# S4 convolution with a gated FFN on Trainium2: the first transform of the convolution in eight array tiles instead of four

## The chip, the cores and the metric

The kernel runs on one core of one Trainium2 chip. The metric is the device time of one execution in microseconds, the median of three runs. The engines are named as in the profile: PE is TensorE (its matmuls), PEld its weight loads, DVE VectorE, ACT ScalarE, POOL GpSimd, SP SyncE, which here only issues DMAs.

## The reference

Two branches read the same normalized input; their product is added to the input.

```python
def reference(A_u, ...):                       # u: (1, 2048, 512)
    xn = _layernorm(A_u, axis=-1)
    s = _A_ref(xn, ...)                        # S4: y = causal convolution over the sequence
    g = _silu(_B_ref(xn, w1, b1, w2, b2))      # gelu(xn @ w1 + b1) @ w2 + b2, 512 -> 1792 -> 512
    return A_u + s * g

def _A_ref(u, ...):
    P = jnp.exp(logdA[:, :, None] * l[None, None, :])
    K = jnp.einsum("dn,dnl,dn->dl", Cc, P, dB).real      # a kernel of 2048 taps for each of 512 channels
    ...                                                  # rfft of K and u, padded to 4096, product, irfft
    return y + u * Dskip
```

## The kernel before

The sequence has 2048 rows of 512 channels; channels are handled in four batches `b` of 128. Three pieces of work are interleaved.

*The start.* `prologue()` loads the first rows of the input and the first weights, computes the time steps, and normalizes. While loads are under way PE multiplies the identity with itself (`warm`, L431, called with 6 and with 25, each a matmul of 128x128 by 128x128 into a bank of tag `f1`). The first work of PE that others wait for are the transposes `xT` of the normalized rows (`ln_turn`, L369); ACT and DVE split them into a high and a low part (`xh`, `xl`), and with these the first layer of the FFN begins (`first_start`, L266).

*The middle.* A long table of tokens, `ORDER`, sets by hand the order in which the FFN's matmuls (`f` L256 to L258, `z` L295 to L297, in a form of fp32 that takes one pass) and the generation of the convolution's taps follow one another. The taps are summed by `gen_sum` (L656), calls with 32 columns of weights and 64 moving columns in four tiles of columns.

*The end.* The convolution is done with two short transforms in place of the FFT: `first_dft` (over 32 points), `second_dft` (L883, over 64), a product, and the way back (`back_dft` L918, `swing` L936, `last_dft` L975). `first_dft` is called with a batch `b`, `u` (0 the input, 1 the taps) and a half `h`, 16 calls in all, here called groups. Its operands lie with 32 rows for each of four sub-batches `g`, so a call of `PE.matmul` has 32 rows, and the four `g` use four tiles of rows of the array and four PSUM banks. The stationary operand is the data (two channels by 64 points: 128 columns), the moving one the constant `fc` (64 columns). ACT, at the first four groups DVE too, copies the four banks out as `X` (`first_out`, L870).

The groups of batch 0 are strung between the last parts of the FFN by a string of tokens (`F00`, `F01`, `F10`, `F11` among `S`, `L` and `A`). Those of batches 1 to 3 stand in `slot(b, g)`, eight slots for each batch: every slot has one `second_dft`, every even slot of batches 0 to 2 one group of the next batch, every odd slot from the first pair on two `back_dft`. From slot to slot PE's work is in the order of the code. Tables of the transforms (`mc`, `tcn`) are loaded by SP's queue around the start of this part.

In fp32 each call of `PE.matmul` becomes two pairs of a weight load and a matmul, so 32 calls stand as x64 in the profile.

Of the kernel before, what the change touches and what calls it, by code (L numbers as in the profile page):

```python
# [11 lines left out]
F32 = mybir.dt.float32  # L12
# [8 lines left out]
P = 128  # L21
# [12 lines left out]
TB = 4  # L34
# [138 lines left out]
def kernel(  # L173
# [5 lines left out]
    V, A, GP, PE, SY = nc.vector, nc.scalar, nc.gpsimd, nc.tensor, nc.sync  # L179
# [27 lines left out]
    fc = keep.tile([P, 2 * N1], F32, name="fc")  # L207
    ident = keep.tile([P, P], F32, name="ident")
# [6 lines left out]
    def stage_first(f):  # L215
        if f >= FA and f % 2:
            x = wka.tile([P, 2, D], F32, tag="x", name=f"ws{f}", bufs=2)
            st, raw_w[f, 1] = x[:, 0, :].rearrange("p (k m) -> p k m", k=KD), x[:, 1, :]
        else:
            st = stg.tile([P, KD, P], F32, tag="st", name=f"w1s{f}")  # L220
        raw_w[f, 0] = st
        SY.dma_start(st, w1.rearrange("(k p) f -> p k f", p=P)[:, :, f * P:(f + 1) * P])

    def stage_second(f):
        if (f, 1) not in raw_w:
            raw_w[f, 1] = stg.tile([P, D], F32, tag="st", name=f"w2s{f}")
        SY.dma_start(raw_w[f, 1], w2[f * P:(f + 1) * P, :])

    def split(f, k, other=0):
        if k == 0:  # L230
            g = f % FA
            W[f] = (wpa.tile([P, KD, P], F32R, tag=f"w1h{g}", name=f"w1h{f}"),
                    wpa.tile([P, KD, P], F32R, tag=f"w1l{g}", name=f"w1l{f}"),
                    wpa.tile([P, D], F32R, tag=f"w2h{g}", name=f"w2h{f}"),
                    wpa.tile([P, D], F32R, tag=f"w2l{g}", name=f"w2l{f}"))
        j = k % 2
        h, lo = W[f][2 * j:2 * j + 2]
        if k < 2:
            A.copy(h, raw_w[f, j])  # L239
        else:  # L240
            (GP if other else V).tensor_sub(lo, raw_w[f, j], h)  # L241

    def opened(stack, name, side, bufs=1, space=None):
        kw = {} if space is None else {"space": space}
        return stack.enter_context(tc.tile_pool(name=name, bufs=bufs, side=side, reuse_waits="tile", **kw))
# [62 lines left out]
    ps1 = opened(fa, "ps1", "left", space=PSUM)  # L308
# [5 lines left out]
    def ln_load(n):  # L314
        if n == 2:
            ln["zi"] = wka.tile([P, TB, D], F32, tag="zi", name="x23")
        if n in (2, 3):
            x = ln["zi"][:, 2 * n - 4:2 * n - 2, :]
        else:
            x = wka.tile([P, 2, D], F32, tag="x", name=f"x{n}", bufs=2)  # L320
        for j in range(2):
            SY.dma_start(x[j * 64:(j + 1) * 64], x_l[j, :, 2 * n:2 * n + 2, :])
        ln[n] = x
# [6 lines left out]
    def ln_stats(n, mv):  # L330
        for i in range(2):
            ln_stat(n, i, mv)
# [16 lines left out]
    def ln_scale(n, mv, rs):  # L349
        x = ln[n]  # L350
        for i in range(2):
            V.tensor_scalar(x[:, i, :], x[:, i, :], mv[:, i, 0:1], rs[:, i:i + 1],
                            op0=ALU.subtract, op1=ALU.mult)
# [18 lines left out]
    def ln_high(n, i, other=0):  # L372
        t, hf = divmod(n, 2)
        s = slice((2 * hf + i) * P, (2 * hf + i + 1) * P)
        if other:
            V.tensor_copy(xt[t][0][:, :, s], ln[n, i])
        else:
            A.copy(xt[t][0][:, :, s], ln[n, i])
# [30 lines left out]
    def bias_load():  # L409
        SB["b2"] = st = wka.tile([P, TB * P], F32, tag="hf", name="b2st", bufs=2)  # L410
        V.memset(st, 0.0)
        for k in (0, 32):
            A.dma_start(st[k:k + 1], b2.rearrange("(o d) -> o d", o=1))
        one = wka.tile([P, TB * P], F32, tag="hf", name="one", bufs=2)
        V.memset(one[:, :P], 1.0)
        A.activation(one[:, P:P + 1], one[:, :1], AF.Gelu_apprx_tanh)
        A.copy(ones, one[:, :P])

    def bias_high():
        A.copy(b2r, SB["b2"])  # L420

    def bias_low():
        V.tensor_sub(b2r[32:33], SB["b2"][32:33], b2r[32:33])
# [4 lines left out]
    def warm(n):  # L428
        p = ps1.tile([P, P], F32, tag="f1", name="warm", bufs=2)
        for _ in range(n):  # L430
            PE.matmul(p, ident, ident, start=True, stop=True, skip_group_check=True)  # L431

    def z_add(t, i):
        V.tensor_add(fin[t][:, i, :], zt[t + NTB][i], fin[t][:, i, :])

# [19 lines left out]
    def timestep():  # L455
        def small(tag, dt=F32):
            return par.tile([P, G], dt, tag=tag, name="sm_" + tag)

        x = small("x")
        rows = par.tile([G, P], F32, tag="pr", name="sm_rows")  # L460
        A.dma_start(rows, log_dt.rearrange("(g p) -> g p", p=P))
        yield
        p = pss.tile([P, G], F32, tag="sm", name="sm_turn")
        PE.transpose(p, rows, ident[:G, :G])
        A.copy(x, p)
        yield
        k, r, t, e = small("k"), small("r"), small("t"), small("e")
        GP.tensor_scalar(x, x, -87.0, 88.5, op0=ALU.max, op1=ALU.min)
        GP.tensor_scalar(k, x, 1.4426950408889634, MAGIC, op0=ALU.mult, op1=ALU.add)
        GP.tensor_scalar(k, k, MAGIC, 1.0, op0=ALU.subtract, op1=ALU.mult)  # L470
        GP.tensor_scalar(t, k, -0.693359375, 1.0, op0=ALU.mult, op1=ALU.mult)
        GP.tensor_add(r, t, x)
        GP.tensor_scalar(t, k, 2.12194440054690583e-4, 1.0, op0=ALU.mult, op1=ALU.mult)
        GP.tensor_add(r, r, t)
        GP.tensor_scalar(e, r, 1.0 / 5040.0, 1.0 / 720, op0=ALU.mult, op1=ALU.add)
        for c in (1.0 / 120, 1.0 / 24, 1.0 / 6, 0.5, 1.0, 1.0):
            GP.tensor_mul(e, e, r)
            GP.tensor_scalar(e, e, c, 1.0, op0=ALU.add, op1=ALU.mult)
        k2 = small("k2", I32)
        GP.tensor_scalar(k2, k, 127.0, 8388608.0, op0=ALU.add, op1=ALU.mult)  # L480
        SB["dt"] = dt = small("dt")
        GP.tensor_mul(dt, e, k2.bitcast(F32))
        yield
# [193 lines left out]
    def prologue():  # L677
        step = timestep()
        next(step)
        ln_load(0)  # L680
        ln_load(1)
        stage_first(0)
        stage_second(0)
        bias_load()
        warm(6)
        next(step)
        warm(25)
        for _ in step:
            pass
        SY.dma_start(b1s, b1.rearrange("(f p) -> p f", p=P))  # L690
        stage_first(1)
        stage_second(1)
        next(pgen[0])
        for n in range(2, 4):
            ln_load(n)
        SY.dma_start(cbs, cb)
        mv, rs = pair(0)
        bias_high()
        ln_stats(0, mv[:, 0:2, :])
        bias_low()  # L700
        ln_stats(1, mv[:, 2:4, :])
        split(0, 0)
        split(0, 1)
        ln_root(0)
        for n in range(2):
            ln_scale(n, *moments(n))
        for q, tag in enumerate(("ph", "sm", "z", "z")):
            ln_turn(q // 2, q % 2, tag)
            ln_high(q // 2, q % 2)
            ln_low(q // 2, q % 2)  # L710
            if q == 1:
                split(0, 2)
        first_start(*steps[0])

    def pair(t):
        if (t, "mv") not in ln:
            ln[t, "mv"] = wka.tile([P, TB, 2], F32, tag="mv", name=f"mv{t}", bufs=2)
            ln[t, "rs"] = wka.tile([P, TB], F32, tag="rs", name=f"rs{t}", bufs=2)
        return ln[t, "mv"], ln[t, "rs"]

    def moments(n):
        s = slice(2 * (n % 2), 2 * (n % 2) + 2)
        mv, rs = pair(n // 2)
        return mv[:, s, :], rs[:, s]

    def ln_root(n):
        ln_rsqrt(*pair(n // 2), str(n))
# [128 lines left out]
    def first_dft(b, u, h, gs):  # L856
        if b not in xf:
            xf[b] = SB["pf" if b % 2 == 0 else "pm"].tile([P, 2, 2, N1, N2], F32, tag=f"X{b % 2}", name=f"X{b}")
        src = side[b][u][h]
        ps = [bank(f"s1_{b}_{u}_{h}_{g}").rearrange("p e (i m) -> p (e i) m", m=N2) for g in gs]  # L860
        for i in range(8):
            for g, p in zip(gs, ps):
                r = slice(g * N1, (g + 1) * N1)
                PE.matmul(p[:, i, :], src[r, 2 * i:2 * i + 2, :], fc[r], start=True, stop=True, skip_group_check=True)  # L864
        fp[b, u, h] = list(zip(gs, ps))

    def first_out(b, u, h, engs=(A, A, A, A)):
# [152 lines left out]
    def slot(b, g):  # L1020
# [15 lines left out]
        if nxt and g % 2 == 0:  # L1036
            first_dft(b + 1, i // 2, i % 2, range(G))
# [57 lines left out]
    with tc.manual_schedule():  # L1095
# [9 lines left out]
        for p in "S0 F00 S1 S2 F01 S3 L0 F10 L1 A0 F11 A1 L2 L3 A2 A3".split():  # L1105
            if p[0] == "F":
                k = int(p[1]), int(p[2])
# [67 lines left out]
```

## Time and profile before

| | us |
|---|---|
| three runs | 566.54, 571.05, 569.23 |
| median | 569.23 |
| span of the profiled execution, first to last instruction | 564.4 |
| PE busy | 543.8 |
| DVE busy | 457.0 |
| ACT busy | 411.5 |
| POOL busy | 297.6 |

The page gives the profiled execution's span; the median of the runs is 4.8 us longer than it. A busy time is the union of an engine's instructions; PE's ends are modelled, so a high share says that PE always has something under way, not that it runs at its best. "issue" as the end of a wait means that no semaphore and no earlier instruction explains it. Counts of instructions (x) in rows of windows include those that reach into the window.

### The profile page before, as it was taken

The numbers are of one execution on the slowest core, as the hardware profiler recorded it, in microseconds if no ns is written. First come the engines' busy times: TensorE is split into PE (matmuls) and PEld (weight loads), VectorE is DVE, ScalarE is ACT, GpSimd is POOL, SyncE is SP. The second block draws the span as 40 slices with busy tenths as digits, with TensorE's granted clock in tenths as the row PEclk, the third lists the DMA queues.
The fourth block names the chain that finished last, engine by engine and source line by source line (L and its number), as shares of the span: only waits on it lengthen the run. The fifth ranks groups of instructions, "written<-read, shape, count | busy, mean of one in ns | idle before, by whom it ended". The sixth has DMA issues, their size and how long they took to land.

```text
span 564.4 us, 17131 instructions
## 1 busy us (share of the span) xinstructions
PE 543.8 (96%) x7179; PEld 434.5 (77%) x7179; DVE 457.0 (81%) x699; ACT 411.5 (73%) x605; POOL 297.6 (53%) x403
## 2 busy tenths in 40 slices
PE   8898999999999999999999999999999999999995
PEld 8666777777777777777777777777779998988873
DVE  6999999999899789998897976886357656867874
ACT  3587998799977998777998787897355565564542
POOL 4648378449976679969743684370320305114323
PEclk9999999999999999999999999999999999999998
DMA  8967636845192364752258138313978583625945
GB/s 188 281 193 207 186 93 201 240 141 195 54 337 74 107 193 136 257 149 58 44 186 236 52 92 107 110 38 126 362 292 78 132 135 83 174 68 126 207 109 112
DMA packets 108344, 86.91 MB, mean 154 GB/s; under 512 B 44294, under 2 KB 87562, under 8 KB 108268
## 3 DMA queue, kind: packets, MB, share of 16 engines
q1 hardware_dynamic: 97584, 65.37, 44.3%
q0 software_dynamic: 9568, 19.93, 12.0%
q8 instruction: 56, 0.92, 0.7%
q10 hardware_dynamic: 1116, 0.53, 0.4%
q14 instruction: 20, 0.16, 0.1%
HBM read 52.25 MB, written 33.55 MB: 152 GB/s over the span
## 4 chain that ended last, share of the span: by engine, by line
PE 60%; DVE 17%; issue 8%; DMA 7%; ACT 3%; SPq 3%; POOL 2%; POOLq 0%; DVEq 0%; ACTq 0%
PE z L295 8%; PE z L296 7%; PE z L297 7%; PE f L256 7%; PE f L258 7%; PE f L257 6%; PE kg L656 5%; PE s L883 4%; PE s L864 3%; PE ph L595 2%; PE sa L918 2%; DVE ra L609 2%; DVE hl L282 2%; DMA xb<-in_A_u_dram 2%; DMA gb<-gd 1%
## 5 line engine op out<-in xcount | busy, mean ns | idle before, releaser
L618 POOL TENSOR_TENSOR mm<-mm,rc 128x32 f32<-128x32 f32 (+4 forms) x150 | 115.8, 772 | 11.8
L295 PE MATMUL z<-w2h,hh 128*128 128x512 f32 x224 | 97.9, 437 | 0.0
L256 PE MATMUL f<-xh,w1h 128*128 128x512 f32 x220 | 91.4, 415 | 0.1
L297 PE MATMUL z<-w2h,hl 128*128 128x512 f32 x224 | 88.5, 395 | 0.3 <-DVE hl L282 0.3
L296 PE MATMUL z<-w2l,hh 128*128 128x512 f32 x224 | 88.6, 395 | 0.0
L258 PE MATMUL f<-xh,w1l 128*128 128x512 f32 x220 | 87.0, 395 | 1.5 <-DVE w1l L241 1.5
L257 PE MATMUL f<-xl,w1h 128*128 128x512 f32 x220 | 86.7, 394 | 0.0
L883 PE MATMUL s<-X,mc 64*64 64x128 f32 x2048 | 63.8, 272 | 1.4 <-issue 1.4
L900 DVE TENSOR_TENSOR t<-s,uh 128x512 f32<-128x512 f32 x64 | 41.0, 685 | 26.6 <-ACT uh L891 26.3
L883 PEld LDWEIGHTS s<-X,mc 64*64 64x64 f32 x2048 | 56.1, 133 | 5.6 <-issue 3.3
L615 POOL COPY mm<-rc 128x32 f32<-128x32 f32 x30 | 14.1, 469 | 81.5 <-DVE e L648 48.9
L282 DVE TENSOR_TENSOR hl<-hf,hh 128x512 fp32r<-128x512 f32 x56 | 49.9, 894 | 5.6 <-ACT hh L276 5.6
L609 DVE SCALAR_TENSOR_TENSOR ra<-ra,ph 128x512 f32<-128x512 f32 x64 | 43.6, 681 | 8.9 <-ACT ra L603 7.9
L258 PEld LDWEIGHTS f<-xh,w1l 128*128 128x128 f32 x220 | 41.3, 188 | 12.3 <-DVE w1l L241 2.4
L270 ACT ACTIVATE hf<-f,b1s 128x512 f32<-128x512 f32 x56 | 38.2, 688 | 17.1 <-DVE hl L282 9.8
L297 PEld LDWEIGHTS z<-w2h,hl 128*128 128x128 f32 x224 | 42.1, 188 | 11.1 <-DVE hl L282 1.2
L295 PEld LDWEIGHTS z<-w2h,hh 128*128 128x128 f32 x224 | 42.5, 190 | 10.5 <-issue 1.0
L256 PEld LDWEIGHTS f<-xh,w1h 128*128 128x128 f32 x220 | 41.5, 189 | 9.8 <-ACT w1h L239 0.3
L296 PEld LDWEIGHTS z<-w2l,hh 128*128 128x128 f32 x224 | 42.3, 189 | 8.2 <-DVE w2l L241 0.2
L257 PEld LDWEIGHTS f<-xl,w1h 128*128 128x128 f32 x220 | 41.4, 188 | 9.0
L641 DVE TENSOR_TENSOR e<-mm,ra 128x1024 f32<-128x1024 f32 x32 | 42.9, 1340 | 5.8 <-ACT ra L629 3.3
L870 ACT COPY X<-s 128x512 f32<-128x512 f32 x56 | 28.9, 598 | 25.3 <-PE s L864 20.2
(185 smaller groups left out, 1163.6 us busy)
## 6 DMA issues: line engine op xcount, KB each, us to landing
x<-in_A_u_dram SPq DMA_DIRECT2D x16, 256.0 KB
xs<-x SPq DMA_DIRECT2D x16, 256.0 KB
xt_h<-xh POOLq DMA_DIRECT2D x4, 1024.0 KB, 5.4
xt_l<-xl POOLq DMA_DIRECT2D x4, 1024.0 KB, 7.4
kgd<-ko SPq DMA_DIRECT2D x32, 128.0 KB
za<-zo SPq DMA_DIRECT2D x4, 1024.0 KB
xh<-xt_h POOLq DMA_DIRECT2D x4, 1024.0 KB, 6.7
xl<-xt_l POOLq DMA_DIRECT2D x4, 1024.0 KB, 10.1
```

The costliest lines, as they stand in the source:

```text
L256: PE.matmul(p, wh[:, k, :], xh[:, k, :], start=(k == 0), stop=False)
L257: PE.matmul(p, wh[:, k, :], xl[:, k, :], start=False, stop=False)
L258: PE.matmul(p, wl[:, k, :], xh[:, k, :], start=False, stop=(k == KD - 1))
L282: V.tensor_sub(hl, hf, hh)
L295: PE.matmul(z, hh[:, s], wh, start=(f0 == 0 and not rows), stop=False)
L296: PE.matmul(z, hh[:, s], wl, start=False, stop=False)
L297: PE.matmul(z, hl[:, s], wh, start=False, stop=(f0 == FA - 1))
L609: V.scalar_tensor_tensor(ra[:, 0, c], ra[:, 1, c], MAGIC, p, op0=ALU.subtract, op1=ALU.subtract)
L618: GP.tensor_mul(mv[:, :, 0:3:2, w:2 * w], mv[:, :, 0:3:2, 0:w], rc[:, 2 + 2 * i:4 + 2 * i, :].rearrange("p j c -> p c j").unsqueeze(3).to_ ...
L641: V.tensor_mul(e1, m1.unsqueeze(1).to_broadcast([P, 2, CH, N1]), ra[:, :, :, :N1])
L883: PE.matmul(p[ka * 64:(ka + 1) * 64, r, o, :, jj], mc[h, k, ((0, 2), (1, 0))[c][o], :], xf[b][h, c, :, k, :], start=(c == 0), stop=(c == 1 ...
L900: V.tensor_mul(t, p[:, i, :, 1].unsqueeze(1).to_broadcast([P, 2, 2, P]), uh)
```

## The change

The groups of `first_dft` use half the columns in each call: a call covers one channel instead of two, 64 columns of weights, and writes one half of the bank's partitions (`p[64 * e:64 * e + 64, i, :]`). Row and column tiles together make eight tiles of 32 rows by 64 columns. A group has 64 calls instead of 32. What is computed, the banks and the copies out of them are the same.

In `prologue()`, 19 of the 25 later warm-up calls are replaced by 256 calls in four tile forms (`warm_tiles`: 5 x 16 in tiles of 32x32, 8 x 8 in 64x32, 8 x 8 in 32x64, 6 x 8 in 64x32 with 128 moving columns); they write banks of tag `z`, which nobody reads.

```diff
+    def warm_tiles(rows, cols, n, k):
+        banks = [ps1.tile([P, n], F32, tag="z", name=f"warm{rows}x{cols}_{r}", bufs=TB) for r in range(P // rows)]
+        for _ in range(k):
+            for c in range(0, P, cols):
+                for r, p in enumerate(banks):
+                    s = slice(r * rows, (r + 1) * rows)
+                    PE.matmul(p[c:c + cols], ident[s, c:c + cols], ident[s, :n], start=True, stop=True, skip_group_check=True)
...
         warm(6)
         next(step)
-        warm(25)
+        warm(6)
+        warm_tiles(32, 32, 128, 5)
+        warm_tiles(64, 32, 64, 8)
+        warm_tiles(32, 64, 64, 8)
+        warm_tiles(64, 32, 128, 6)
+        warm(4)
...
         for i in range(8):
             for g, p in zip(gs, ps):
                 r = slice(g * N1, (g + 1) * N1)
-                PE.matmul(p[:, i, :], src[r, 2 * i:2 * i + 2, :], fc[r], start=True, stop=True, skip_group_check=True)
+                for e in range(2):
+                    PE.matmul(p[64 * e:64 * e + 64, i, :], src[r, 2 * i + e, :], fc[r], start=True, stop=True, skip_group_check=True)
```

The order of PE's calls at the start of the program before the change. Names are the tile that is written, then what is read; `x4` is four calls of one kind.

```order
L431 MATMUL warm_149<-ident_99 128x128 x6
L464 MATMUL sm_turn_156<-ident_99,sm_rows_129 128x4
L431 MATMUL warm_159<-ident_99 128x128 x25
L369 MATMUL xT0_0_276<-ident_99,x0_131 128x128 x4
L369 MATMUL xT0_1_283<-ident_99,x0_131 128x128 x4
L369 MATMUL xT1_0_291<-ident_99,x1_134 128x128 x4
L369 MATMUL xT1_1_298<-ident_99,x1_134 128x128 x4
```

The changed program at its start, first calls of the first tile form:

```order
L431 MATMUL warm_149<-ident_99 128x128 x6
L472 MATMUL sm_turn_156<-ident_99,sm_rows_129 128x4
L431 MATMUL warm_159<-ident_99 128x128 x6
L439 MATMUL warm32x32_0_166<-ident_99 32x128
L439 MATMUL warm32x32_1_167<-ident_99 32x128
L439 MATMUL warm32x32_2_168<-ident_99 32x128
L439 MATMUL warm32x32_3_169<-ident_99 32x128
```

And its last ones, up to the first transposes:

```order
L439 MATMUL warm64x32_1_385<-ident_99 32x128
L439 MATMUL warm64x32_0_384<-ident_99 32x128
L431 MATMUL warm_434<-ident_99 128x128 x4
L369 MATMUL xT0_0_530<-ident_99,x0_131 128x128 x4
L369 MATMUL xT0_1_537<-ident_99,x0_131 128x128 x4
```

Between the second `warm` and the transposes stand 260 calls in place of 19; the transposes themselves are the same.

PE around the first slot before the change: the end of the FFN, one `second_dft` (`s2`, 32 calls) and the beginning of a group (`s1`, 32 rows of this kind, which read `fc` and the input `in0` of batch 1).

```order
L296 MATMUL z7_3_4571<-w2l13_2978,hh_7_13_4979 128x512
L297 MATMUL z7_3_4571<-w2h13_2977,hl_7_13_4983 128x512
L883 MATMUL s2_0_0_5240<-X0_5029,mc_5006 64x2x64 x32
L864 MATMUL s1_1_0_0_0_5274<-fc_98,in0_1_5018 128x64
L864 MATMUL s1_1_0_0_1_5275<-fc_98,in0_1_5018 128x64
L864 MATMUL s1_1_0_0_2_5276<-fc_98,in0_1_5018 128x64
L864 MATMUL s1_1_0_0_3_5277<-fc_98,in0_1_5018 128x64
```

The same place after it:

```order
L897 MATMUL s2_0_0_5622<-X0_5283,mc_5260 64x2x64 x32
L878 MATMUL s1_1_0_0_0_5656<-fc_98,in0_1_5272 64x64 x2
L878 MATMUL s1_1_0_0_1_5657<-fc_98,in0_1_5272 64x64 x2
L878 MATMUL s1_1_0_0_2_5658<-fc_98,in0_1_5272 64x64 x2
L878 MATMUL s1_1_0_0_3_5659<-fc_98,in0_1_5272 64x64 x2
```

Each row of a group has become two calls of half the width; what stands before and behind the group is unmoved. On the other engines no instruction is added, removed or moved.

## The prediction

> **What bounds the kernel now.** I read first the busy times and the chain on the page, then the busy time of each engine by stage.
>
> ```profile
> PE 543.8 (96%) x7179; PEld 434.5 (77%) x7179; DVE 457.0 (81%) x699; ACT 411.5 (73%) x605; POOL 297.6 (53%) x403
> PE 60%; DVE 17%; issue 8%; DMA 7%; ACT 3%; SPq 3%; POOL 2%; POOLq 0%; DVEq 0%; ACTq 0%
> q8 instruction: 56, 0.92, 0.7%
> 0.00:12.40 12.40, 10.36 (x63) 9.93 (x63) 6.84 (x25) 3.69 (x7) 5.78 (x29) 1.00 0.86 189
> 12.40:20.40 8.00, 5.74 (x31) 4.26 (x31) 7.90 (x18) 5.54 (x11) 4.08 (x7) 1.00 0.97 268
> 40.00:392.00 352.00, 347.15 (x3337) 267.22 (x3338) 314.49 (x448) 302.30 (x406) 233.03 (x299) 1.00 0.52 146
> 392.00:411.20 19.20, 18.05 (x350) 14.50 (x348) 7.01 (x12) 7.12 (x12) 4.37 (x4) 1.00 0.90 332
> 411.20:512.60 101.40, 99.97 (x2577) 90.66 (x2576) 66.62 (x98) 58.78 (x109) 19.97 (x20) 1.00 0.59 131
> ```
>
> The columns of a stage are PE, PEld, DVE, ACT, POOL, the granted clock, the DMA share and GB/s. The first transform (L864) runs from 392 to 511, where PE is busy all but 2.6 us while DVE and ACT have a third or more of the stage free. So PE's order of work sets the end there, and also from 40 to 392. Only at the start does PE wait for others: behind the first transposes DVE is busy 7.90 of 8.00 us.
>
> Next the time line of PE, for what one group of the first transform costs and for waits that belong to no engine.
>
> ```profile
> 392.76 1.10 PE L656 MATMUL kg<-e,e 128*32 128x64 f32 x64
> 393.80 0.50 PE L295 MATMUL z<-w2h,hh 128*128 128x512 f32 x1
> ...
> 411.22 1.96 PE L883 MATMUL s<-X,mc 64*64 64x128 f32 x58
> 413.52 0.44 PE L883 MATMUL s<-X,mc 64*64 64x128 f32 x6 [0.34 <-issue]
> 413.89 2.01 PE L864 MATMUL s<-fc,in 32*128 32x64 f32 x64
> 415.84 1.96 PE L883 MATMUL s<-X,mc 64*64 64x128 f32 x58
> 418.72 2.19 PE L883 MATMUL s<-X,mc 64*64 64x128 f32 x70 [0.93 <-issue]
> 420.84 2.01 PE L864 MATMUL s<-fc,in 32*128 32x64 f32 x64
> 422.78 1.98 PE L883 MATMUL s<-X,mc 64*64 64x128 f32 x64
> 424.69 2.05 PE L918 MATMUL sa<-tcn,Y 128*128 128x128 f32 x16
> 426.67 1.98 PE L883 MATMUL s<-X,mc 64*64 64x128 f32 x64
> ```
>
> A call in fp32 is two pairs of a weight load and a matmul in the trace: 32 calls of a group are x64. From start to start a group of L864 takes 422.78-420.84 = 1.94 us, and two slots take 426.67-418.72 = 7.95 us. Twice PE stood still in the middle of L883, in a run with no semaphore of its own, "issue". The stages between these gaps, and the packets on the queue that brings instructions (windows 410.99 to 411.00 and 416.32 to 416.33), say what it waited for.
>
> ```profile
> 407.28:413.51 6.23, 5.90 (x128) 5.05 (x128) 3.46 (x6) 4.83 (x8) 0.23 (x1) 1.00 1.01 409
> 413.51:418.71 5.20, 4.27 (x128) 3.79 (x127) 1.29 (x2) 2.64 (x5) 3.27 (x5) 1.00 1.03 376
> 418.71:422.39 3.68, 3.67 (x126) 3.50 (x126) 2.50 (x4) 1.17 (x2) 0.00 (x0) 1.00 0.36 117
> 451.74:455.65 3.91, 3.91 (x138) 3.67 (x133) 2.82 (x5) 1.93 (x4) 0.00 (x0) 1.00 0.49 134
> q8 instruction: 1, 0.02, 751.2%
> q8 instruction: 1, 0.02, 673.8%
> ```
>
> From one gap's end to the next are 128 matmuls and 128 weight loads, 256 instructions. q8 moved 0.92 MB in 56 packets, 16 KB each; 56 x 256 = 14,336, and PE has 2 x 7179 = 14,358 instructions: q8 feeds PE, 256 instructions at a time. The packet that began at 411.0 took 7.512 x 16 x 0.01 = 1.20 us, was there at 412.2, and PE went on at 413.52, 1.3 us later. The one of 416.3 took 1.08, was there at 417.4, and PE went on at 418.72, again 1.3 us later. It began 2.8 us after PE had entered the block before (413.52). So only the running block and the next are held: entering one block sends for the next but one. A block of 128 pairs cannot pass faster than this round: 6.2 and 5.2 us where the DMA share is 1.0, 3.7 to 3.9 where it is 0.4 to 0.5. The present code needs 64 x 30 ns x 2 = 3.9 us for 128 pairs of L883 and L864, just at that limit.
>
> [...]
>
> **The change, part by part.** *Time of a group without the fetch.* In how tiles overlap I rely on these:
>
> ```profile
> L883 PEld LDWEIGHTS s<-X,mc x2048: 129/133/133, 411.2 to 543.1; 64*64 64x64 f32 x187
> L864 PEld LDWEIGHTS s<-fc,in x1024: 181/187/187, 392.4 to 510.6; 32*128 32x128 f32 x171
> 420.83:420.86 0.03, 0.02 (x4) 0.03 (x4) 1.00 0.00 0
> 420.86:420.94 0.08, 0.08 (x4) 0.08 (x4) 1.00 0.01 0
> ```
>
> The four row tiles get their four pairs within 0.03 us, then none starts until 420.94: PE sits out the load of 128 columns. A group is 16 rounds of 1.94/16 = 121 ns. Halving the columns shortens a load by 187-133 = 54 ns. The nearest row for small weights and the same 64 moving columns is L656: 64 pairs in 393.80-392.76 = 1.04 us, 65 ns a round. Eight pairs at 0.03/4 = 7.5 ns fit in 60 ns. So a group costs 1.04 to 1.1 us, if pairs can keep coming at 7.5 ns. No row shows eight tiles side by side; if they ran four at a time, or pairs came no faster than L656's 16 ns, 128 pairs would take 2.08. Between -0.90 and +0.14 us I take -0.85, from the 0.03 us row. DVE and ACT have the room named above, so they would not be next; instructions would.
>
> [...]
>
> *Fetch in the slots, 411 to 513 (12 groups).* Two slots hold 64+64+64+16 = 208 pairs now and 272 after, 1.63 and 2.13 blocks. At a round of 3.8 us (between 3.7 and 3.9) 2.13 blocks need 8.1 us even if work and fetch average out perfectly. They don't: the block with the 16 pairs of L918 has 112 x 0.030 + 2.0 = 5.3 us of work, and the other 1.13 blocks 4.3 us of fetch, 9.6 together. Halfway is 8.85 against 7.95, +0.9 for two slots, 12 times: **+10.8 us**. Ends: -10.2 (12 x -0.85, fetch hidden) and +19.8 (9.6 for two slots).
>
> *Fetch in the four groups before the slots, 392 to 411.* The row of this stage has 350+348 = 698 instructions in 19.2 us, 2.7 blocks at 7.0 us each, a little above the rounds of 6.2 and 5.2 us that end in and behind it. One of its four groups waited for ACT besides:
>
> ```profile
> 395.39 2.01 PE L864 MATMUL s<-fc,in 32*128 32x64 f32 x62
> 400.08 2.66 PE L864 MATMUL s<-fc,in 32*128 32x64 f32 x64 [1.09 <-ACT X L870]
> ```
>
> The groups bring 256 pairs more, two blocks: 4.7 blocks at 5.2 us are 24.6 us, +5.4, and at 6.2 us 29.3, +10. I take **+5**, by the lower row, as a block may be there at the stage's begin. Ends: -3.4 (4 x -0.85, rounds under 3.4 us) and +10.
>
> *The warm-up.* 31 calls become 272, 62 pairs 544: 964 instructions more ahead of the first transpose, on which ACT, DVE and all of the FFN wait.
>
> ```profile
> 1.51 2.93 PE L431 MATMUL warm<-ident 128*128 128x128 f32 x12 [1.51 <-POOL ident masks.py:199]
> 4.56 7.31 PE L431 MATMUL warm<-ident 128*128 128x128 f32 x50
> 12.46 2.17 PE L369 MATMUL xT<-ident,x 128*128 128x128 f32 x16 [0.59 <-DVE x L352]
> q8 instruction: 1, 0.02, 61.5%
> ```
>
> The last row is the first packet of q8, between 20.4 and 20.5; up to there PE ran (63+31) x 2 = 188 instructions. So about 190 instructions and one block of 256 are there from the start. The transposes begin behind 126 instructions now, behind 1,090 after: 126+964. That is beyond 190 + 3 x 256 = 958: three blocks must be fetched, one after the other. The first 12 pairs take 2.63 us (0.22 each), so do the 12 behind L464's successor: tiles begin at 4.56+2.6 = 7.2 and instruction 190 comes at 7.9. Then three rounds, then 132 instructions (58 tile pairs at 16 ns, 8 pairs at 0.11): 1.8 us. The transposes start at 9.7 + 3 rounds. A round is unknown here: 2.5 if the packet starts at once (1.2 + 1.3), 3.7 as at DMA share 0.36, 6.2 as at 1.01; the share at the start is 0.86 to 0.97. I take 4.5, a little under the midpoint of the last two (5.0), as the packet at 20.4 began within a few instructions of the entry that sent for it. That gives 23.2 against 12.46, +10.7, of which DVE's full stage gives next to nothing back: **+10.5**, ends +4.7 and +15.8. If the forms keep the clock from rising (0.22 us a pair at first, 7.31/50 = 0.15 in the mean of the second run), up to 3 us are added; I take none. The z banks that the tile forms write have no reader, so nobody waits for them.
>
> *Sum.* 10.8 + 5 + 10.5 = 26.3 on the span of 564.4: 590.7. The three times' median of 569.23 lies 4.8 above that span: 595.
>
> **The rivals.** (a) *Fetch is hidden, the group's 0.85 us is kept*: 16 x 0.85 = 13.6, and the tile forms at 7.5 ns a pair end near 12: 556. For it: most of the 56 blocks show no gap. Against: blocks took 12 us in the FFN and meet the limit wherever they take 4. It decides if a round in the slots falls below 7.1/2.13 = 3.3 us and the start holds more than one block. Faster; 0.08. (b) *Only the warm-up pays*: rounds near 3.5, so the slots break even: 580; 0.15. (c) *Only the stage pays*, because the start has further blocks ready: 585; 0.06. (d) *The two cancel*, slots at PE's own pace (-10.2) and the warm-up at +10.5: 569; 0.05.
>
> **How the numbers follow.** The forecast, all three terms, has 0.66. With rounds from 3.5 to 4.1 in the slots and 3.7 to 6.2 at the start it spans about 582 to 611. Down to 577 (b) and (c) lie inside; (a), (d) and a tenth of the forecast's own cases stay out, together 0.2. So 577 to 611. Slower by over 1% (about what a measurement of this kernel tells from no change): 0.66+0.15+0.06 = 0.87. Within 1%: 0.05. Faster: 0.08.
>
> **What would show it.** Right: the first transpose near 23 us with two or three "issue" gaps of 2 to 4 us in the tile forms of the warm-up; q8 with 11 or 12 packets more (3,012 instructions / 256), three of them before the first transpose; L864 in two or more pieces per group with "issue" gaps; two slots of 8.5 to 9.5 us; a PE that is busy less. Wrong: a first transpose at 12.5; a group that runs through in 1.1 us and two slots of 7.1 us, which is (a); or 128 pairs in over 1.9 us without a gap, which would put the price on the pairs themselves and not on the fetch.

## The result, and the profile after

| | before | after |
|---|---|---|
| runs | 566.54, 571.05, 569.23, 565.52 | 607.96, 609.40, 609.59, 607.99 |
| median, us | 567.88 | 608.69 |
| span of the profiled execution, us | 564.4 | 606.2 |

The changed kernel takes 1.073 times as long, 95% interval 1.068 to 1.078: 40.8 us more. The page of the changed kernel, its lines on the engines' busy times, the granted clock, PE's instruction queue, and the two transforms (`second_dft` is now L897, `first_dft` L878):

```profile
PE 557.6 (92%) x8685; PEld 443.0 (73%) x8685; DVE 458.3 (76%) x699; ACT 411.8 (68%) x605; POOL 297.2 (49%) x403
PEclk9799999999999999999999999996699999798999
q8 instruction: 68, 1.11, 0.8%
L897 PE MATMUL s<-X,mc 64*64 64x128 f32 x2048 | 70.9, 288 | 8.1 <-issue 8.1
L878 PE MATMUL s<-fc,in 32*64 32x64 f32 x2048 | 31.6, 249 | 18.0 <-issue 18.0
```

The other engines do what they did. PE has 1506 pairs more, q8 brings 12 blocks more, PE's busy share falls from 96 to 92%, and 26 us of idle time stand before the two transforms alone with "issue" as the end: time for which the profile shows no engine and no DMA that PE waited for. The clock, at 0.9 or more before in every slice but the last, stands at 0.6 to 0.8 in five of the 40 slices.

The time line of PE at the start of the changed kernel, the tile forms of the warm-up up to the first transposes:

```profile
6.90 2.32 PE L439 MATMUL warm32x<-ident 32*32 32x128 f32 x160
9.23 0.67 PE L439 MATMUL warm64x<-ident 64*32 64x64 f32 x38
11.70 1.11 PE L439 MATMUL warm64x<-ident 64*32 64x64 f32 x90 [1.80 <-issue]
12.74 0.84 PE L439 MATMUL warm32x<-ident 32*64 32x64 f32 x38
15.15 1.72 PE L439 MATMUL warm32x<-ident 32*64 32x64 f32 x90 [1.57 <-issue]
16.80 1.53 PE L439 MATMUL warm64x<-ident 64*32 64x128 f32 x38
20.25 1.94 PE L439 MATMUL warm64x<-ident 64*32 64x128 f32 x58 [1.92 <-issue]
22.12 1.72 PE L431 MATMUL warm<-ident 128*128 128x128 f32 x8
23.68 1.91 PE L369 MATMUL xT<-ident,x 128*128 128x128 f32 x16
```

Between the three gaps lie 90+38 = 128 pairs each time, 256 instructions. A gap falls in the middle of a form, not where forms change. The transposes begin at 23.68 instead of 12.46. The instruction queue's packets stand where the prediction looked for them, here the ones that began at 9.00 and at 415.02 (windows 9.00 to 9.01 and 415.02 to 415.03):

```profile
q8 instruction: 1, 0.02, 818.1%
q8 instruction: 1, 0.02, 594.4%
```

They took 1.31 and 0.95 us and had landed at 10.31 and 415.97; PE went on at 11.70 and, in the next rows, at 417.46, 1.4 and 1.5 us later. The second began 4.0 us after PE had entered the block before it (410.99). The stage before the slots and the first slots show the same:

```profile
406.62 1.41 PE L878 MATMUL s<-fc,in 32*64 32x64 f32 x106
410.99 0.44 PE L878 MATMUL s<-fc,in 32*64 32x64 f32 x18 [2.96 <-issue]
...
413.32 1.98 PE L878 MATMUL s<-fc,in 32*64 32x64 f32 x104
417.46 0.70 PE L878 MATMUL s<-fc,in 32*64 32x64 f32 x24 [2.16 <-issue]
...
433.50 3.34 PE L897 MATMUL s<-X,mc 64*64 64x128 f32 x64
436.77 1.60 PE L878 MATMUL s<-fc,in 32*64 32x64 f32 x128
438.30 0.88 PE L897 MATMUL s<-X,mc 64*64 64x128 f32 x23
441.18 3.16 PE L897 MATMUL s<-X,mc 64*64 64x128 f32 x105 [2.00 <-issue]
```

And by windows of the changed kernel (columns as before): the stage before the slots, the slots up to the last group, and two stretches from one gap's end to the next.

```profile
403.70:433.50 29.80, 21.14 (x604) 15.89 (x603) 7.14 (x11) 7.55 (x13) 4.62 (x6) 0.70 0.75 290
433.50:551.80 118.30, 101.26 (x3281) 90.25 (x3280) 65.99 (x97) 58.12 (x107) 19.30 (x18) 0.94 0.43 92
410.99:417.46 6.47, 4.31 (x129) 3.23 (x129) 1.29 (x2) 1.08 (x2) 3.96 (x4) 0.61 1.02 414
417.46:424.51 7.05, 5.27 (x127) 3.94 (x128) 1.98 (x3) 1.07 (x2) 0.66 (x3) 0.63 1.02 409
```

The same two stages of the kernel before:

```profile
392.40:411.22 18.82, 17.67 (x348) 14.46 (x347) 6.75 (x11) 7.12 (x12) 4.37 (x4) 1.00 0.92 339
411.22:510.70 99.48, 98.05 (x2513) 88.89 (x2512) 66.35 (x98) 57.08 (x105) 19.97 (x20) 1.00 0.60 131
```

So the loss is 11.2 us at the start (23.68 - 12.46), 11.0 before the slots (29.80 - 18.82) and 18.8 in them (118.30 - 99.48): 41.0 of the 41.8 by which the spans differ. Behind the last group 54.4 us follow in place of 53.7. Most of what is lost in the two stages is idle time of PE, by these rows 7.5 of the 11.0 and 15.6 of the 18.8 us; the rest is longer busy time. The shorter matmuls are seen where no block ends inside a group: 438.30 - 436.77 = 1.53 us in place of 1.94.

### The profile page after: what moved, and what is told of

It is laid out like the page before. It is cut to its first block, busy times and chain, and to the rows that moved or that the text cites. A ratio compares the mean times of both kernels' runs of the same rounds, so it can differ in the third digit from the quotient of the medians.

```text
span 606.2 us, 20145 instructions
## 1 busy us (share of the span) xinstructions
PE 557.6 (92%) x8685; PEld 443.0 (73%) x8685; DVE 458.3 (76%) x699; ACT 411.8 (68%) x605; POOL 297.2 (49%) x403
## 4 chain that ended last, share of the span: by engine, by line
PE 68%; DVE 19%; issue 8%; ACT 3%; POOL 1%; DVEq 0%; POOLq 0%; ACTq 0%
PE s L897 10%; PE z L295 7%; PE z L296 6%; PE z L297 6%; PE f L256 6%; PE f L258 5%; PE f L257 5%; PE s L878 5%; PE sa L932 5%; PE kg L664 4%; PE w L950 2%; DVE hl L282 2%; PE ph L603 2%; DVE ra L617 2%; DVE e L653 1%
## 5 line engine op out<-in xcount | busy, mean ns | idle before, releaser
L626 POOL TENSOR_TENSOR mm<-mm,rc 128x32 f32<-128x32 f32 (+4 forms) x150 | 113.6, 757 | 11.8
L897 PE MATMUL s<-X,mc 64*64 64x128 f32 x2048 | 70.9, 288 | 8.1 <-issue 8.1
L897 PEld LDWEIGHTS s<-X,mc 64*64 64x64 f32 x2048 | 61.8, 143 | 13.0 <-issue 11.2
L282 DVE TENSOR_TENSOR hl<-hf,hh 128x512 fp32r<-128x512 f32 x56 | 51.2, 917 | 5.3 <-ACT hh L276 5.3
L258 PEld LDWEIGHTS f<-xh,w1l 128*128 128x128 f32 x220 | 41.3, 188 | 12.8 <-DVE w1l L241 3.0
L905 ACT COPY uh<-s 128x512 f32<-128x512 f32 x32 | 18.7, 585 | 43.4 <-issue 21.2
L878 PE MATMUL s<-fc,in 32*64 32x64 f32 x2048 | 31.6, 249 | 18.0 <-issue 18.0
```

The lines of the kernel that those rows point to most:

```text
L258: PE.matmul(p, wl[:, k, :], xh[:, k, :], start=False, stop=(k == KD - 1))
L282: V.tensor_sub(hl, hf, hh)
L626: GP.tensor_mul(mv[:, :, 0:3:2, w:2 * w], mv[:, :, 0:3:2, 0:w], rc[:, 2 + 2 * i:4 + 2 * i, :].rearrange("p j c -> p c j").unsqueeze(3).to_ ...
L878: PE.matmul(p[64 * e:64 * e + 64, i, :], src[r, 2 * i + e, :], fc[r], start=True, stop=True, skip_group_check=True)
L897: PE.matmul(p[ka * 64:(ka + 1) * 64, r, o, :, jj], mc[h, k, ((0, 2), (1, 0))[c][o], :], xf[b][h, c, :, k, :], start=(c == 0), stop=(c == 1 ...
```

## The experiments

Each was compared with the kernel before on the same chip. The theory, an inference from the rows above, is that PE waits for its instructions: two blocks of 256 are held (at the start 446 instructions, 223 pairs, ran before the first gap, about 190 and one block, then 256 from gap to gap), and a third is sent for once the second is entered (a packet that began at 415.02, behind the entry at 410.99 and ahead of the one at 417.46).

**Each half of the change alone.** `e1_warm_only` has the new warm-up and the old transform, `e2_tiles_only` the reverse.

```diff
 # e1_warm_only, against the changed kernel
-                for e in range(2):
-                    PE.matmul(p[64 * e:64 * e + 64, i, :], src[r, 2 * i + e, :], fc[r], ...)
+                PE.matmul(p[:, i, :], src[r, 2 * i:2 * i + 2, :], fc[r], ...)
 # e2_tiles_only, against the changed kernel
-        warm(6)
-        warm_tiles(32, 32, 128, 5)
-        ...
-        warm(4)
+        warm(25)
```

> The warm-up of the changed kernel alone; the first transform as before (four tiles of 32 by 128). Fetch theory: three blocks of 256 instructions have to come, one after the other, before the first transpose, as in the changed kernel: first transpose at 23 to 24 us instead of 12.5, gaps of 1.5 to 2 us at the same three places of the tile forms, and all of that delay kept to the end: 568 + 11 = 579 us (577 to 582). Rival A, that the loss of the changed kernel sits in the eight-tile form of the transform and the late start is caught up later, as PE waits for DVE there anyway: 568 to 571.

> The first transform in eight tiles alone; the warm-up as before. Fetch theory: first transpose at 12.5 us, first group near 392, then the changed kernel's losses of 11 us before the slots and 19 us in them: 568 + 30 = 598 us (594 to 601), with gaps of 1.5 to 3 us inside the groups, each at a block's end of 256 instructions. Rival B, that the stage suffers from what the long start brings (a later, denser DMA load, a clock that has dropped): under 585.

Measured: `e1_warm_only` 580.70 us, 1.023 times the kernel before (1.017 to 1.029), so 13 us more; `e2_tiles_only` 592.87 us, 1.045 (1.039 to 1.051), 25 us more. Together 38, nearly the whole. The time line of `e1_warm_only` has the gaps at the same places and the transposes at 24.0 us, where they take 3.08 us in place of 1.91:

```profile
11.98 1.29 PE L439 MATMUL warm64x<-ident 64*32 64x64 f32 x90 [2.26 <-issue]
15.44 1.71 PE L439 MATMUL warm32x<-ident 32*64 32x64 f32 x90 [1.25 <-issue]
20.26 1.94 PE L439 MATMUL warm64x<-ident 64*32 64x128 f32 x58 [1.65 <-issue]
24.00 3.08 PE L369 MATMUL xT<-ident,x 128*128 128x128 f32 x16
```

Rival A falls: the late start is not caught up. So does rival B in the main: with the start as before, the two stages still lose most, though not all. Windows of `e2_tiles_only`, the two stages:

```profile
393.40:420.28 26.88, 20.98 (x605) 15.70 (x604) 7.23 (x11) 7.56 (x13) 4.78 (x6) 0.75 0.84 321
420.28:533.60 113.32, 99.16 (x3281) 88.04 (x3280) 65.49 (x97) 57.09 (x105) 19.73 (x18) 0.97 0.43 96
```

8.1 us are lost before the slots (26.88 - 18.82) and 13.8 in them, less than the 11.0 and 18.8 of the whole change, and with a higher clock (0.75 against 0.70, 0.97 against 0.94). The expected 598 (594 to 601) was the sum of the whole change's losses; the time lies 5 us below it and outside the range.

**A tile form inside what is held at the start.** `e3_warm_resident` keeps the tiles of 32 by 32 and makes up the rest of the time with full calls; the transform is the old one.

```diff
         warm(6)
         warm_tiles(32, 32, 128, 5)
-        warm_tiles(64, 32, 64, 8)
-        warm_tiles(32, 64, 64, 8)
-        warm_tiles(64, 32, 128, 6)
-        warm(4)
+        warm(14)
```

> The warm-up with one tile form only (80 calls in tiles of 32 by 32) between 12 and 14 full calls; the first transform as before. The first transpose then stands at about instruction 430, inside what is held at the start (about 190 and one block of 256). Fetch theory: no gap in the tile form, first transpose at 12.4 to 12.7 us, time as before, 568 us (565 to 571). Rival C, that tile forms in themselves start the FFN late or cold (switching forms, a clock that doesn't rise): first transpose over 14 us or matmuls of 512 columns at twice 0.23 us apart behind it, 572 or more.

Measured: 567.13 us, 1.000 (0.996 to 1.004). Its time line has no gap:

```profile
7.38 2.32 PE L439 MATMUL warm32x<-ident 32*32 32x128 f32 x160
9.63 3.39 PE L431 MATMUL warm<-ident 128*128 128x128 f32 x28
12.86 1.91 PE L369 MATMUL xT<-ident,x 128*128 128x128 f32 x16
```

160 pairs in sixteen tiles, a change of form on both sides, and the transposes stand at 12.86 (0.2 later than the expected range; the tiles began at 7.38, in the changed kernel at 6.90). Rival C falls: in this run the form cost nothing by itself (1.000).

**Eight tiles with as few instructions as before.** In `e4_tiles_few` each call moves the 64 columns of the constant twice and so fills two places of the bank; every second pair of channels gets its neighbours' values.

```diff
                 for e in range(2):
-                    PE.matmul(p[64 * e:64 * e + 64, i, :], src[r, 2 * i + e, :], fc[r], ...)
+                    if i % 2 == 0:
+                        PE.matmul(p[64 * e:64 * e + 64, i:i + 2, :], src[r, 2 * i + e, :],
+                                  fc[r].unsqueeze(1).to_broadcast([N1, 2, 2 * N1]), ...)
```

> The first transform in the same eight tiles, but with as many instructions as before: 32 calls a group, each with 128 moving columns (the 64 of the constant twice), so that every second pair of channels gets its neighbours' values; the warm-up as before. Fetch theory: a group costs 0.9 to 1.1 us in place of 1.94 and has no more gaps than before; 16 groups give up to 14 us, less what the fetch of 1.6 blocks for two slots then takes back: 555 to 563 us. Rival D, that the eight-tile form itself stalls (a drain at each change of form, tiles that run four at a time, PSUM banks): gaps in the groups as in the changed kernel or groups of 1.8 us or more, 568 to 598.

Measured: 560.56 us, 0.988 (0.983 to 0.993). Its time line in the slots (`first_dft` is L866 there):

```profile
412.99 0.44 PE L885 MATMUL s<-X,mc 64*64 64x128 f32 x6 [1.06 <-issue]
413.36 1.21 PE L866 MATMUL s<-fc,in 32*64 32x128 f32 x64
414.50 1.96 PE L885 MATMUL s<-X,mc 64*64 64x128 f32 x58
417.64 2.19 PE L885 MATMUL s<-X,mc 64*64 64x128 f32 x70 [1.18 <-issue]
...
421.18 0.44 PE L866 MATMUL s<-fc,in 32*64 32x128 f32 x7 [0.28 <-issue]
```

And the window of its slots:

```profile
409.96:504.20 94.24, 89.97 (x2513) 78.60 (x2512) 65.52 (x97) 57.83 (x106) 20.44 (x20) 1.00 0.61 139
```

A group of the same eight tiles takes 1.14 us, 0.80 less than before, and the gaps of the kernel before stand at the same places, longer (1.06 and 1.18 against 0.34 and 0.93) as PE reaches the block's end sooner. No more gaps than before were expected, but others follow behind these, the one at 421.18 inside a group. With groups of 1.14 us rival D falls. Of 16 x 0.80 = 12.8 us only about 6.5 arrive (0.0116 x 566). In the slots, where 12 groups save 9.6 us, the stage is 5.2 us shorter (99.48 - 94.24), and PE's idle time there has grown from 1.4 to 4.3 us: part of what the array saves goes to the fetch even at the old count of instructions.

**Half the instructions at the old array time.** `e5_wide` goes the other way: 64 rows and 128 columns, a block-diagonal constant, 16 calls a group.

```diff
-        for i in range(8):
-            for g, p in zip(gs, ps):
-                r = slice(g * N1, (g + 1) * N1)
-                PE.matmul(p[:, i, :], src[r, 2 * i:2 * i + 2, :], fc[r], ...)
+        for i in range(8):
+            for q in range(2):
+                r = slice(q * 64, (q + 1) * 64)
+                PE.matmul(ps[q, i // 4][:, i % 4, :], src[r, 2 * i:2 * i + 2, :], fc[r], ...)
...
-            d, p = xf[b][:, :, u, :, 16 * g + 8 * h:16 * g + 8 * h + 8], p.rearrange("p i (c k) -> p c k i", c=2)
+            d = xf[b][:, :, u, :, 32 * q:32 * q + 32].rearrange("p c k (g x) -> p g c k x", g=2)
+            p = p.rearrange("p i (g c k) -> p g c k i", g=2, c=2)
+            d = d[:, :, :, :, 8 * h + 4 * ih:8 * h + 4 * ih + 4]
```

> The first transform with half the instructions of before at the same array time: 64 rows and 128 columns in two tiles, the moving constant made block-diagonal (128 columns, half of them zeros) so that one call serves two sub-batches; 16 calls a group, 32 pairs; the copies out read the banks in another order. Fetch theory: a group still takes 1.8 to 1.95 us, the gaps of 0.3 and 0.9 us that the kernel before has at blocks' ends go, and the stage before the slots is no longer near the fetch: 1 to 4 us less than before, 562 to 567. Rival, that the number of instructions only hurts through the eight-tile form: same as before within 1 us; slower than before if the copies out with their extra dimension cost ACT more than now.

Measured: 562.73 us, 0.994 (0.992 to 0.997), 3.3 us less than before (2.9 by the medians): little, but the interval leaves out 1, and it is faster than both kernels. Its page's line on q8 (packets, MB, share):

```profile
q8 instruction: 52, 0.85, 0.7%
```

Its time line in the first slots (`first_dft` is L867):

```profile
413.95 2.06 PE L867 MATMUL s<-fc,in 64*128 64x128 f32 x32
415.93 2.72 PE L889 MATMUL s<-X,mc 64*64 64x128 f32 x89
418.85 1.32 PE L889 MATMUL s<-X,mc 64*64 64x128 f32 x39 [0.19 <-issue]
```

And the window of its slots:

```profile
412.04:509.80 97.76, 97.57 (x2129) 88.41 (x2128) 66.09 (x98) 58.18 (x107) 19.86 (x20) 1.00 0.58 134
```

A group takes 1.98 us (413.95 to 415.93), 0.04 more than before. Of the gaps 0.19 us is left here where 0.34 and 0.93 stood; the slots are 1.7 us shorter (99.48 - 97.76), and 1.2 of that is idle time of PE (1.43 against 0.19).

**The data in the slots.** What makes a round of the fetch long? `e6_before_quiet` and `e7_tiles_quiet` are the kernel before and `e2_tiles_only` without the loads of gate and input (POOL writes zeros instead) and without the stores of batches 0 to 2 in the slots.

```diff
-            tail_load(b - 1, when.index(g))
+            t = gx[b - 1, when.index(g)] = gx.pop((b - 1, when.index(g), "t"), None) or new_tail(b - 1, when.index(g))
+            for x in t:
+                GP.memset(x, 0.0)
...
             xb = gx.pop((b, 2 * t + h))[1]
+            if b < NB - 1:
+                continue
```

> The kernel before without the loads of gate and input (replaced by POOL's memsets) and without the stores for batches 0 to 2 in the slots, so that the output of these batches is missing; it is the measure for the next run. Both theories: PE sets the pace in the slots, so 0 to 8 us less than before, 558 to 566.

> The eight-tile transform (warm-up as before) with the same DMAs left out, output of batches 0 to 2 missing. Theory Q: the round of the fetch in the slots is long because its packet waits behind data, so without these DMAs rounds shrink from 3.5 to 6 us toward 3.5, and the loss in the slots from 14 us to under 7; in all 8 to 17 us above the quiet kernel before (the stage before the slots keeps its 8 to 9). Rival F: the round is the sequencer's own and doesn't depend on the data: still 22 to 27 us above the quiet kernel before.

Measured: `e6_before_quiet` 564.76 us, 0.998 (0.996 to 1.000); `e7_tiles_quiet` 584.45, 1.034 (1.029 to 1.038). The second lies 19.7 us above the first, between what the two theories expected. A trace of the first that could be set beside the others is not on record. Window of the slots of `e7_tiles_quiet`:

```profile
419.60:531.00 111.40, 99.29 (x3281) 88.51 (x3280) 66.36 (x97) 57.24 (x105) 26.73 (x34) 0.96 0.26 51
```

The DMA share falls from 0.43 to 0.26, and the slots from 113.32 to 111.40 us. The rounds that stopped PE there, each counted from 128 pairs before the gap's end, are as long as before: 2.5 to 5.6 us in `e2_tiles_only` and 2.5 to 5.4 in `e7_tiles_quiet`, 3.5 in the mean of 13 both times. The longest of each, `e2_tiles_only` first:

```profile
458.52:464.15 5.63, 3.42 (x128) 2.99 (x127) 3.14 (x6) 2.64 (x5) 0.45 (x2) 1.00 0.82 218
455.91:461.27 5.36, 3.42 (x148) 2.99 (x131) 3.38 (x6) 2.65 (x6) 1.70 (x5) 1.00 0.36 133
```

So these DMAs are not what makes the rounds long, and theory Q is not borne out. Between the two profiled executions (588.3 and 583.3 us) lie 5.0 us: 1.9 in the slots (113.32 - 111.40), 2.4 behind the last group, 1.2 ahead of the first, less 0.5 in the stage before the slots. Whether a round is all the sequencer's own stays open, since tables and inputs are still loaded here.

## Why the prediction was right, and where it was short

The forecast was slower, 595 us within 577 to 611; the time is 608.69. The direction and the mechanism held: twelve blocks more on q8 (11 or 12 said), three gaps in the tile forms with 128 pairs between them, groups in two pieces, PE less busy. Two of the signs came out by kind and not by size: the gaps at the start are 1.6 to 1.9 us where 2 to 4 were said, and two slots take 118.30/12 = 9.9 us where 8.5 to 9.5 were. Rival (a), fetch hidden, falls by `e2_tiles_only`; (b) and (c), one half alone, by the two halves; (d), the two cancel, by their sum.

*The warm-up*: transposes "at 9.7 + 3 rounds" of 4.5 us gave 23.2, and they came at 23.68. That the sum fits so well is in part luck. The three rounds took 12.4 us from the entry at 7.8 to 20.25, not 13.5, and the 66 pairs behind them 3.4 us, not 1.8, at a clock that the sum took as full and that was at half speed to 23.34. `e1_warm_only` keeps the delay to the end, `e3_warm_resident` takes it away with the count of instructions alone.

*The stage before the slots* was mis-sized, +5 said and +11.0 measured. I took the lower of two rows for a round, 5.2 us; the three stretches from one gap's end to the next took 6.47, 7.05 and 5.30 (the last ends at 429.81), 6.3 in the mean. The upper row, 6.2, gave +10. The reason I gave for the lower, a block that may be there at the stage's begin, was worth one round of five at most.

*The slots*: +10.8 said, +18.8 measured (+13.8 without the new warm-up). The step that was mis-sized is the average of 8.85 us for two slots, halfway between perfect evening out and none: measured is 18.8/12 = +1.6 us for two slots where +0.9 was said (13.8/12 = +1.15 without the new warm-up), nearer to none. The round of 3.8 in it was not a measured round: no gap ends at 422.39 or 455.65, so the rows of 3.68 and 3.91 show PE's own work and only that a round is no longer than that. The rounds that stopped PE in the slots of the changed kernel went from 2.6 to 6.2 us; that their mean is 3.9 is luck.

*The group* was mis-sized too, though the +10.8 doesn't use it; it carries rivals (a) and (d) and the lower ends. I took 1.04 to 1.1 us from four pairs that start within 0.03 us. Four of the six groups of the slots that no gap cuts take 1.53 us, 12 ns a pair, between the 0.03 us row and L656's 16 ns a pair (2.08). The burst is real but short, as a window with the matmuls and weight loads of this group alone (PE, PEld, clock, DMA) shows:

```profile
436.77:437.00 0.23, 0.23 (x25) 0.23 (x32) 1.00 0.98 285
```

Of the group's 128 loads 32 begin in its first 0.23 us; the other 96 take 1.3. Why the pace falls is not shown.

*The last term*, 4.8 us from the span to the median, was 2.5 (608.69 - 606.2).

*The clock* was named as up to 3 us at the start and taken as none. That the tile forms keep it from rising was not shown: in the kernel before it was granted at 1.00 from 0 to 20.4 us, so the pace of 0.22 and then 0.15 us a pair there shows no clock that rises. In the changed kernel the granted clock was 0.50 in three stretches of 10.24 us, one at the start (13.10 to 23.34) and two that began before the slots (412.46 to 422.70 and 426.12 to 436.36), and in shorter ones within the slots (484.14 to 487.55 and 518.27 to 525.10). The first of them:

```profile
13.10:23.34 10.24, 6.75 (x225) 5.60 (x212) 0.67 (x2) 0.00 (x0) 2.77 (x6) 0.50 0.86 244
```

`second_dft` at 433.50 took 3.27 us, mostly at 0.50, for what takes 1.91 (451.93 to 453.84) at 1.00. The stage before the slots ran at 0.70 of the clock in the whole change and 0.75 in `e2_tiles_only`, the slots at 0.94 and 0.97; the two lost 29.8 and 21.9 us there. But of these 7.9 us 5.6 are idle time of PE (25.7 against 20.1) and only 2.3 longer busy time. The slower clock is seen in longer matmuls (those of 512 columns start 0.42 us apart at 419.54 and 419.96, 0.23 at 411.93 and 412.16); that it lengthens the waits for blocks is shown nowhere. No run changed the clock by itself, so its share is argued, not shown, and why the waits came out longer with the new warm-up than without it stays open. The four runs of `e2_tiles_only` also differ among themselves by 4.7 us, and its profiled one is the shortest.

## What to carry to other kernels

Before splitting matmuls into more and smaller tiles, count instructions: here PE stood still with "issue" where 128 pairs of weight load and matmul had less work than the round in which their block came, 2.5 to 7.05 us, and behind some of these gaps the granted clock was 0.50. In stages that are near that limit the better direction here was fewer and larger calls, even with zeros in the constant (`e5_wide`, 0.994), and filler ahead of the first real work cost no time where it fitted in what is held at the start (`e3_warm_resident`: 426 instructions ahead of the transposes at 12.86 us, 1.000); where it did not, the transposes came 11.2 us late (1,090 instructions, 23.68 us). Gaps that come every 256 instructions in the middle of a run, with no semaphore, and an instruction queue whose packet lands 1.3 to 1.5 us before PE goes on, are the mark to look for.

## What was not expected of the hardware

The granted clock was at half speed behind a wait much shorter than a stage: in `e4_tiles_few` a wait of 2.47 us for ACT before a group was followed by 3.42 us at 0.50, in which matmuls of 512 columns ran 0.42 us apart. From 406.20 on they ran 0.23 us apart again, and in the slots (409.96 to 504.20) the granted clock was 1.00. That the wait brought the clock down is not shown.

```profile
399.94 1.91 PE L866 MATMUL s<-fc,in 32*64 32x128 f32 x64 [2.47 <-ACT X L872]
402.80 0.63 PE L297 MATMUL z<-w2h,hl 128*128 128x512 f32 x1
403.22 0.63 PE L295 MATMUL z<-w2h,hh 128*128 128x512 f32 x1
401.44:404.86 3.42, 3.42 (x29) 2.08 (x24) 1.41 (x3) 1.07 (x2) 2.83 (x3) 0.50 1.00 387
```

The length of a gap did not decide it. In the changed kernel the granted clock stayed at 1.00 from 441.18 to 457.80, with gaps of 1.70 and 1.80 us in that stretch, and was at 0.50 from 484.14 to 487.55, behind a gap of 1.40 us that ended at 483.51.

And PE started four pairs within 0.03 us but needed 1.53 us for a group's 128, about 12 ns a pair, so eight tiles of 64 columns saved 0.4 us of 1.94 in a group, not 0.85, before any fetch.
